# Retention plus Fourier mixing on one core: the order of seven products, and their sums and stores, in the last batch's second weight multiplication

## The chip, the core and the metric

The kernel runs on one core of a Trainium2 chip. A core has a matrix engine (TensorE, PE in the profile; its weight loads are PEld), three engines for element-wise work (VectorE is DVE, ScalarE is ACT, GpSimd is POOL), a fifth that mostly issues DMAs (SyncE, SP), a large on-chip memory (SBUF) and a small one into which TensorE accumulates (PSUM, in banks). Each engine works through its own queue in order and waits on semaphores for the others. POOL does not touch PSUM in this kernel. The metric is the time of one execution in microseconds (us); a kernel's time is the median of its runs.

## The reference

Two stages. The first is a linear attention with a decay per head, over 4 batches, 8 heads, 768 steps and head size 64; the second takes its output as 4 sequences of 768 rows of 512:

```python
for t in range(S):
    state = gamma * state + einsum('bhd,bhe->bhde', k[:, :, t], v[:, :, t])
    y[:, :, t] = scale * einsum('bhd,bhde->bhe', q[:, :, t], state)
...
X = np.fft.fft(np.fft.fft(x, axis=1), axis=2)
u = x + np.real(X)
un = (u - mean(u)) / sqrt(var(u) + 1e-06)
out = u + np.maximum(un @ w_ch1, 0.0) @ w_ch2
```

w_ch1 is 512 x 2048, w_ch2 is 2048 x 512. Only the last line, in the last of the four batches, is touched by the change: the multiplication of the hidden layer by w_ch2 and the adding of u.

## The kernel before

The batches go through a software pipeline: while one batch's feed-forward ("majors") runs on PE, the attention and the Fourier transforms of the next one are woven in between. `emit` (L1233) sorts the units of all streams by a due time between b and b+1 and traces them in that order; for each engine, the compiler keeps about that order and may take an instruction earlier when it reckons the one in front not to be ready.

In the last batch there is no next one. Its 768 rows are taken in three groups p = 0, 1, 2 of 256 rows, and each is 8 hidden units (`h3_unit`, L1032) and then 7 products (`p3_unit`, L1066): 45 majors, the n-th due at n/45 of the batch. Beside them run the last three row blocks (128 rows each) of the batch's own Fourier transform and norm, at the due times MIX3 (L40): `s2_unit` (matmuls L838, ACT copies L840 and L841, DVE L845 and L848, POOL L875 and L877), `norm_unit` (DVE bn_stats L895 and L896, a square root on ACT L898), `scaled_unit` (DVE L912 and L913, ACT L916) and `unT_unit` (a transposing DMA on SP, L938). Group 0 has the fifth row block's norm beside its products. The sixth block's `s2_unit` comes between group 0's last product and group 1's first hidden unit, its norm just ahead of group 1's third hidden unit.

A hidden unit n is 16 matmuls of 256 columns (L1039) into one of three PSUM banks (`ps_pm`) and a relu to f16 into `ht16`, rows n and n + 8: on ACT (L1044) for all n but 2, on DVE (L1046) for n = 2. After units 3 and 7 DVE makes four sums of hidden blocks each (L1063).

The multiplication by w_ch2 is done with seven products in place of eight quarter products. A group's hidden rows are A11, A12 (first 128 rows; first and second 1024 hidden columns) and A21, A22 (second 128 rows); w_ch2 is B11, B12, B21, B22 in the same way, each 1024 x 256. With

```
S1 = A21 + A22   S2 = S1 - A11   S3 = A11 - A21   S4 = A12 - S2
T1 = B12 - B11   T2 = B22 - T1   T3 = B22 - B12   T4 = B21 - T2
P1 = A11 B11   P2 = A12 B21   P3 = S4 B22   P4 = A22 T4   P5 = S1 T1   P6 = S2 T2   P7 = S3 T3
w = P1 + P6
o11 = u11 + P1 + P2            o12 = u12 + w + P5 + P3
o21 = u21 + w + P7 + P4        o22 = u22 + w + P7 + P5
```

S1 to S4 are the tiles `hsum` and T1 to T4 the tiles `wsum` (made once, ahead). Each product is 8 matmuls (L1096), weights from the hidden side. PSUM banks come from `ps_g` (5 banks): P1 and P2 accumulate in bank a, P5 and P3 in bank d; b, c and e are P6's, P7's and P4's.

The sums: w is copied from bank a by ACT (L1100) after P1; DVE adds P4 to u21 in place (L1115), P2 to u11 giving o11 (L1102), P6 to w (L1119); then POOL adds w to u22, u21 and u12 in place, in this order (L1121); DVE adds P5 to u22 in place (L1117), P7 to u22 and u21 giving o22 and o21 (L1123, L1124), and the content of d after P3 to u12 giving o12 (L1109). o11 and o12 are one tile of 512 columns, o21 and o22 another.

The order of the products is in `PROD` (L43): 1, 4, 2, 6, 5, 7, 3 in the first two groups, 1, 4, 6, 5, 7, 3, 2 in the last. In the last group bank a is two banks with 128 columns each: P1 and P2 are then 16 matmuls of 128 columns, with their ACT copy and DVE add in halves.

Stores: in the first two groups one of 512 columns for the first row block (L1113, after P3) and one for the second (L1125, after P7), on SP's queue. In the last group the second row block still goes in one piece (L1125), o12 on SP (L1111), and o11 in two halves, the first on ACT's queue and the second on SP's (L1105). L1331 holds the program's closing waits.

Of the kernel before, what the change touches and what calls it, by code (L numbers as in the profile page):

```python
# [12 lines left out]
ALU = mybir.AluOpType  # L13
# [5 lines left out]
P = 128  # L19
B, H, S, D = 4, 8, 768, 64  # L20
DM = 512
# [18 lines left out]
MIX3 = ((0.005, 0.035, 0.070, 0.105), (0.190, 0.310, 0.325, 0.350), (0.355, 0.395, 0.420, 0.470))  # L40
WS = (0.7, 1.05)
H3_ACT = (0, 1, 3, 4, 5, 6, 7)
PROD = ((1, 4, 2, 6, 5, 7, 3), (1, 4, 6, 5, 7, 3, 2))  # L43
HS_AT = {3: (0, 4), 7: (4, 8)}
ACT_ROWS = ((2, 5, 6, 7, 8, 9, 10, 14), (0, 3, 6, 7, 9, 10, 11, 12, 14, 15))

# [2 lines left out]
def kernel(  # L49
# [9 lines left out]
    nc = tc.nc  # L59
# [276 lines left out]
    for j in range(2):  # L336
        x = const.tile([P, NCH, 2, XW], f16, tag=f"x16_{j}", name=f"x16_{j}")
# [689 lines left out]
    def wsum(j, f):  # L1027
        return ws[j][:, f, :] if f < 6 else ws["hi", j // 2][:, 2 * (j % 2) + f - 6, :]
# [37 lines left out]
    def p3_unit(p, n):  # L1066
        def run():
            u = lb[B - 1]["u"]
            r0, r1 = 2 * p, 2 * p + 1
            u11, u12 = u[:, r0, 0:256], u[:, r0, 256:DM]  # L1070
            u21, u22 = u[:, r1, 0:256], u[:, r1, 256:DM]
            end = p == 2
            if n == 1:
                pr.clear()
                pr["o"] = [obp.tile([P, DM], f32, tag="ob", name="ob") for _ in range(2)]
                pr["w"] = inp.tile([P, 2, NCH, D], f32, tag="in32", name="ws32").rearrange(
                    "p a c d -> p (a c d)")[:, 0:256]
            o0, o1 = pr["o"]
            o11, o12, o21, o22 = o0[:, 0:256], o0[:, 256:DM], o1[:, 0:256], o1[:, 256:DM]
            w = pr["w"]  # L1080
            bank, first, last, lh, rh = {
                1: ("a", True, False, lambda f: ht16[:, f, 0:P], lambda f: w216[:, f, 0:256]),
                2: ("a", False, True, lambda f: ht16[:, 8 + f, 0:P],
                    lambda f: w216[:, 8 + f, 0:256]),
                3: ("d", False, True, lambda f: hs[3][:, f], lambda f: w216[:, 8 + f, 256:DM]),
                4: ("e", True, True, lambda f: ht16[:, 8 + f, P:256], lambda f: wsum(3, f)),
                5: ("d", True, False, lambda f: hs[0][:, f], lambda f: wsum(0, f)),
                6: ("b", True, True, lambda f: hs[1][:, f], lambda f: wsum(1, f)),
                7: ("c", True, True, lambda f: hs[2][:, f], lambda f: wsum(2, f))}[n]
            cols = ((0, 128), (128, 256)) if bank == "a" and end else ((0, 256),)  # L1090
            if first:
                pr[bank] = [ps_g.tile([P, 256], f32, tag="g", name="psc", padded_shape=[P, DM])
                            for _ in cols]
            for ps, (c0, c1) in zip(pr[bank], cols):
                for f in range(8):
                    nc.tensor.matmul(ps[:, c0:c1], lh(f), rh(f)[:, c0:c1],  # L1096
                                     start=first and f == 0, stop=last and f == 7,
                                     skip_group_check=True)
                if n == 1:
                    nc.scalar.copy(w[:, c0:c1], ps[:, c0:c1])  # L1100
                elif n == 2:
                    nc.vector.tensor_tensor(out=o11[:, c0:c1], in0=ps[:, c0:c1],  # L1102
                                            in1=u11[:, c0:c1], op=ALU.add)
                    if end:
                        (nc.sync if c0 else nc.scalar).dma_start(  # L1105
                            out[B - 1, r0 * P:r0 * P + P, c0:c1], o11[:, c0:c1])
            ps = pr[bank][0]
            if n == 3:
                nc.vector.tensor_tensor(out=o12, in0=ps, in1=u12, op=ALU.add)  # L1109
                if end:  # L1110
                    nc.sync.dma_start(out[B - 1, r0 * P:r0 * P + P, 256:DM], o12)  # L1111
                else:
                    nc.sync.dma_start(out[B - 1, r0 * P:r0 * P + P], o0)  # L1113
            elif n == 4:
                nc.vector.tensor_tensor(out=u21, in0=ps, in1=u21, op=ALU.add)  # L1115
            elif n == 5:
                nc.vector.tensor_tensor(out=u22, in0=ps, in1=u22, op=ALU.add)  # L1117
            elif n == 6:
                nc.vector.tensor_tensor(out=w, in0=ps, in1=w, op=ALU.add)  # L1119
                for x in (u22, u21, u12):  # L1120
                    nc.gpsimd.tensor_tensor(out=x, in0=x, in1=w, op=ALU.add)  # L1121
            elif n == 7:
                nc.vector.tensor_tensor(out=o22, in0=ps, in1=u22, op=ALU.add)  # L1123
                nc.vector.tensor_tensor(out=o21, in0=ps, in1=u21, op=ALU.add)  # L1124
                nc.sync.dma_start(out[B - 1, r1 * P:r1 * P + P], o1)  # L1125
        return run

    def w1_unit(g):
# [125 lines left out]
    for b in range(B):  # L1254
# [14 lines left out]
        else:  # L1269
            for p in range(3):  # L1270
                majors += [h3_unit(p, n) for n in range(8)]
                majors += [p3_unit(p, n) for n in PROD[p == 2]]
        streams.append((majors, b, b + 1.0))
# [8 lines left out]
        if b + 1 < B:  # L1282
# [7 lines left out]
            else:  # L1290
                streams.append(([load_unit(b + 1, i) for i in range(4)], b + LD1[0], b + LD1[1]))
                n = [len(u) for u in steps[1:]]
# [3 lines left out]
            end = b + ts[-1]  # L1296
# [39 lines left out]
```

## Time and profile before

| what | value |
|---|---|
| median of 3 runs | 247.41 us (246.95 to 247.58) |
| the profiled execution | 246.58 us |
| its span, first to last instruction | 244.8 us |
| granted TensorE clock | 1.000 over the span |
| the three runs of 8 hidden units (chain of waits) | 6.99, 6.99 and 7.00 us |
| group 0, 1, 2 of products, PE from P1's start to the last matmul's end | 206.56 to 213.48, 220.54 to 227.22, 234.04 to 240.99 us |
| last store: issue, landing | 241.34 us, 1.7 us later |

A timeline row gives the start, the length, the engine, the line, the operation, what it writes and reads, the shape and how many instructions were merged; in brackets is the time the engine stood idle before it, and what ended that. An engine name with a q is its queue issuing a DMA. PE's instructions overlap: a matmul lasts longer than the time after which the next may start. Times count from the span's start.

### The profile page before, as it was taken

Reading aid. Unit: us, or ns where it says so; the run is one execution under the profiler, and the core shown is the slowest. Engines: PE = TensorE matmul, PEld = TensorE weight load, DVE = VectorE, ACT = ScalarE, POOL = GpSimd, SP = SyncE. Lnnn points to the kernel's source line nnn. Section 1 sums busy time; section 2 is a strip of 40 time slices with the busy share of each in tenths; the row PEclk is TensorE's granted clock in tenths of the full one; section 3 lists DMA queues with packets and bytes.
Section 4 is the critical chain, followed back from the end, with each engine's and each line's share of the span. In section 5 each row is a group of like instructions: output and inputs, shape, how many; then the busy total and the mean of one; then the engine's idle time right before and its main releaser. Section 6 shows DMA issues by size and latency. Waiting matters only on the chain.

```text
span 244.8 us, 5672 instructions
## 1 busy us (share of the span) xinstructions
PE 232.4 (95%) x2160; PEld 156.2 (64%) x2160; DVE 190.7 (78%) x476; ACT 131.1 (54%) x287; POOL 87.8 (36%) x155
## 2 busy tenths in 40 slices
PE   6897899999999998999999999999999999999993
PEld 2454668956766645665567546665666469888882
DVE  8998958897797788996885778899896646865443
ACT  8798679587775444751247515732247527271330
POOL 7667601465600067690000646660003220522112
PEclk9999999999999999999999999999999999999999
DMA  8999999799999487999999467696200241031202
GB/s 176 258 259 144 200 200 203 176 250 266 251 215 225 72 171 176 191 177 149 253 277 215 93 151 201 122 121 139 88 0 1 62 134 21 3 112 21 86 3 87
DMA packets 99355, 36.41 MB, mean 149 GB/s; under 512 B 89856, under 2 KB 96384, under 8 KB 99328
## 3 DMA queue, kind: packets, MB, share of 16 engines
q1 hardware_dynamic: 94960, 31.79, 62.1%
q0 software_dynamic: 4224, 4.19, 10.7%
q8 instruction: 17, 0.28, 0.5%
q14 instruction: 10, 0.08, 0.1%
q10 hardware_dynamic: 144, 0.07, 0.1%
HBM read 27.26 MB, written 6.29 MB: 137 GB/s over the span
## 4 chain that ended last, share of the span: by engine, by line
PE 69%; DMA 8%; DVE 7%; ACT 6%; SPq 4%; POOL 3%; issue 2%; ACTq 0%; POOLq 0%; DVEq 0%
PE psc L997 21%; PE psh L958 18%; PE psh L1039 9%; PE psc L1096 6%; DMA q<-in_q_dram 5%; SPq L170 4%; PE ps L741 3%; PE wkA L605 3%; DMA k<-in_k_dram 3%; PE wkY L659 2%; PE pq L838 2%; PE wkY L655 1%; ACT un L891 1%; PE wkK L624 1%; ACT g L748 1%
## 5 line engine op out<-in xcount | busy, mean ns | idle before, releaser
L997 PE MATMUL psc<-w,ht 128*128 128x512 f16 x288 | 68.2, 379 | 0.0
L958 PE MATMUL psh<-unT,w 128*128 128x384 f16 x320 | 59.7, 326 | 0.0
L875 POOL TENSOR_TENSOR u<-u,x 128x256 f32<-128x256 f32 x21 | 13.4, 640 | 105.3 <-DVE u L845 97.1
L997 PEld LDWEIGHTS <-ht 128*128 128x128 f16 x288 | 27.2, 98 | 26.1 <-issue 0.2
L958 PEld LDWEIGHTS <-w 128*128 128x128 f16 x320 | 29.9, 98 | 15.8 <-issue 0.6
L962 ACT ACTIVATE ht<-psh 128x384 f16<-128x384 f32 x46 | 22.3, 490 | 23.6 <-PE psh L958 23.3
L608 DVE TENSOR_TENSOR atm<-wkA,maskp 128x512 f16<-128x512 f32 x36 | 23.7, 681 | 1.2 <-PE wkA L605 1.2
L1039 PE MATMUL psh<-unT,w 128*128 128x256 f16 x192 | 21.4, 273 | 0.0
L1039 PEld LDWEIGHTS <-w 128*128 128x128 f16 x192 | 18.7, 98 | 2.1
L964 DVE TENSOR_SCALAR ht<-psh 128x384 f16<-128x384 f32 x34 | 18.5, 547 | 1.8 <-PE psh L958 1.7
L895 DVE BATCH_NORM_STATS2 bst<-u 128x6 f32<-128x512 f32 x21 | 14.6, 695 | 6.6 <-POOL u L877 5.9
L1001 DVE SCALAR_TENSOR_TENSOR ob<-psc,stats,u 128x512 f32<-128x512 f32 x18 | 13.4, 744 | 6.5 <-PE psc L997 6.5
L634 DVE SCALAR_TENSOR_TENSOR s<-s,gk,wkK 128x128 f16<-128x128 f16 x48 | 16.3, 340 | 2.7 <-ACT s L630 1.9
L1044 ACT ACTIVATE ht<-psh 128x512 f16<-128x512 f32 x21 | 12.2, 593 | 10.5 <-PE psh L1039 10.4
L667 ACT ACTIVATE x<-wkY,gexp 128x384 f16<-128x384 f32 x24 | 12.8, 582 | 8.0 <-PE wkY L659 8.0
L902 ACT ACTIVATE un<-u,stats 128x512 f16<-128x512 f32 x15 | 10.8, 722 | 11.4 <-DVE stats L896 7.7
L388 POOL TENSOR_SCALAR kd<-k,gexp 128x384 f16<-128x384 f32 x24 | 13.9, 590 | 4.0 <-DMA k<-in_k_dram 4.0
L156 PE MATMUL wps<-ht 128*128 128x512 f16 x40 | 13.1, 433 | 2.2 <-POOL ht L207 2.2
L877 POOL TENSOR_TENSOR u<-u,x 128x256 f32<-128x256 f32 x21 | 13.3, 635 | 3.0 <-DVE stats L896 3.0
L1121 POOL TENSOR_TENSOR u<-u,ws 128x256 f32<-128x256 f32 x9 | 6.3, 728 | 20.6 <-DVE ws L1119 20.6
L605 PE MATMUL wkA<-qTz,kT 128*128 128x256 f16 x72 | 13.4, 273 | 0.1
L840 ACT COPY qn<-pq 128x128 f32<-128x128 f32 x18 | 4.9, 273 | 12.6 <-PE pq L838 12.6
(192 smaller groups left out, 430.3 us busy)
## 6 DMA issues: line engine op xcount, KB each, us to landing
q<-in_q_dram SPq DMA_DIRECT2D x16, 384.0 KB, 6.0
k<-in_k_dram SPq DMA_DIRECT2D x16, 384.0 KB, 5.6
v<-in_v_dram SPq DMA_DIRECT2D x16, 384.0 KB, 6.4
out_dram<-ob SPq DMA_DIRECT2D x23, 256.0 KB, 2.4
w<-in_moe_w_ch_dram POOLq DMA_DIRECT2D x8, 512.0 KB, 11.0
unT<-un SPq DMA_TRANSPOSE x15, 2.4
qTz<-q16z SPq DMA_TRANSPOSE x8, 3.9
kT<-kd SPq DMA_TRANSPOSE x8, 3.1
```

The lines of the kernel that those rows point to most:

```text
L388: kc = nc.gpsimd.tensor_scalar(out=kd[:, :, h2, :], in0=k32[:, h2], scalar1=gkd[:, h0 + h2:h0 + h2 + 1], scalar2=1.0, op0=ALU.mult, op1=AL ...
L605: mm = nc.tensor.matmul(wk[:, c2], st["kT"][:, c, :], st["qT"][:, :, c, :], start=True, stop=True)
L608: nc.vector.tensor_tensor(out=st["atm"][:, 2 * part:2 * part + 2], in0=wk, in1=maskp[:, PAIR_ORDER[i]].unsqueeze(1).to_broadcast([P, 2, 2, ...
L634: nc.vector.scalar_tensor_tensor(out=s16[:, c], in0=s16[:, c - 1], scalar=gk2[:, hp:hp + 1], in1=wk[:, c - c0], op0=ALU.mult, op1=ALU.add)
L875: nc.gpsimd.tensor_tensor(out=u[:, kb, 0:256], in0=u[:, kb, 0:256], in1=x[:, kb, 0, 1:257], op=ALU.add)
L895: nc.vector.bn_stats(bst, u[:, kb, :])
L958: nc.tensor.matmul(psh, w116[:, cb, fb * P:(fb + 1) * P], unT[:, cb, rt * 384:(rt + 1) * 384], start=(cb == 0), stop=(cb == 3))
L962: nc.scalar.activation(ht16[:, fb, :], psh, AF.Relu, bias=0.0, scale=-1.0)
L964: nc.vector.tensor_scalar(out=ht16[:, fb, :], in0=psh, scalar1=-1.0, scalar2=0.0, op0=ALU.mult, op1=ALU.max)
L997: nc.tensor.matmul(psc, ht16[:, fb, rb3 * P:(rb3 + 1) * P], w216[:, fb, :], start=(fb == 0), stop=(fb == NFB - 1))
L1039: nc.tensor.matmul(psh[:, t], w116[:, cb, fb * P:(fb + 1) * P], unT[:, cb, p * 256:(p + 1) * 256], start=(cb == 0), stop=(cb == 3))
L1096: nc.tensor.matmul(ps[:, c0:c1], lh(f), rh(f)[:, c0:c1], start=first and f == 0, stop=last and f == 7, skip_group_check=True)
```

## The change

The orders become 1, 4, 2, 5, 6, 7, 3 in the first two groups (P5 ahead of P6) and 1, 4, 6, 7, 5, 2, 3 in the last (P7 ahead of P5, P2 ahead of P3). In the last group it is now bank d that is in two halves, so P5 and P3 go in 16 matmuls of 128 columns with their DVE adds in halves, and P1 and P2 in 8 of 256. There DVE adds w to u22, where POOL did (POOL keeps u21 and u12), P7 is added to u22 in place, and o22 comes from P5. The last group's quarters are stored one by one: o21 after P7, o22 after P5, o11 after P2 on SP's queue, o12 after P3 in two halves, the first on ACT's queue and the second on SP's. `add` and `store` are new helpers for the same DVE add and DMA as before.

```diff
-PROD = ((1, 4, 2, 6, 5, 7, 3), (1, 4, 6, 5, 7, 3, 2))
+PROD = ((1, 4, 2, 5, 6, 7, 3), (1, 4, 6, 7, 5, 2, 3))
...
-            cols = ((0, 128), (128, 256)) if bank == "a" and end else ((0, 256),)
+            cols = ((0, 128), (128, 256)) if bank == "d" and end else ((0, 256),)
...
+            def add(o, x, y):
+                nc.vector.tensor_tensor(out=o, in0=x, in1=y, op=ALU.add)
+
+            def store(r, c0, c1, src, queue=nc.sync):
+                queue.dma_start(out[B - 1, r * P:r * P + P, c0:c1], src)
+
             for ps, (c0, c1) in zip(pr[bank], cols):
                 for f in range(8):
                     nc.tensor.matmul(ps[:, c0:c1], lh(f), rh(f)[:, c0:c1],
                                      start=first and f == 0, stop=last and f == 7,
                                      skip_group_check=True)
-                if n == 1:
-                    nc.scalar.copy(w[:, c0:c1], ps[:, c0:c1])
-                elif n == 2:
-                    nc.vector.tensor_tensor(out=o11[:, c0:c1], in0=ps[:, c0:c1],
-                                            in1=u11[:, c0:c1], op=ALU.add)
+                if n == 3:
+                    add(o12[:, c0:c1], ps[:, c0:c1], u12[:, c0:c1])
                     if end:
-                        (nc.sync if c0 else nc.scalar).dma_start(
-                            out[B - 1, r0 * P:r0 * P + P, c0:c1], o11[:, c0:c1])
+                        store(r0, 256 + c0, 256 + c1, o12[:, c0:c1], nc.sync if c0 else nc.scalar)
+                elif n == 5:
+                    add((o22 if end else u22)[:, c0:c1], ps[:, c0:c1], u22[:, c0:c1])
             ps = pr[bank][0]
-            if n == 3:
-                nc.vector.tensor_tensor(out=o12, in0=ps, in1=u12, op=ALU.add)
+            if n == 1:
+                nc.scalar.copy(w, ps)
+            elif n == 2:
+                add(o11, ps, u11)
                 if end:
-                    nc.sync.dma_start(out[B - 1, r0 * P:r0 * P + P, 256:DM], o12)
-                else:
-                    nc.sync.dma_start(out[B - 1, r0 * P:r0 * P + P], o0)
+                    store(r0, 0, 256, o11)
             elif n == 4:
-                nc.vector.tensor_tensor(out=u21, in0=ps, in1=u21, op=ALU.add)
-            elif n == 5:
-                nc.vector.tensor_tensor(out=u22, in0=ps, in1=u22, op=ALU.add)
+                add(u21, ps, u21)
             elif n == 6:
-                nc.vector.tensor_tensor(out=w, in0=ps, in1=w, op=ALU.add)
-                for x in (u22, u21, u12):
+                add(w, ps, w)
+                if end:
+                    add(u22, u22, w)
+                for x in (u21, u12) if end else (u22, u21, u12):
                     nc.gpsimd.tensor_tensor(out=x, in0=x, in1=w, op=ALU.add)
             elif n == 7:
-                nc.vector.tensor_tensor(out=o22, in0=ps, in1=u22, op=ALU.add)
-                nc.vector.tensor_tensor(out=o21, in0=ps, in1=u21, op=ALU.add)
-                nc.sync.dma_start(out[B - 1, r1 * P:r1 * P + P], o1)
+                add(u22 if end else o22, ps, u22)
+                add(o21, ps, u21)
+                if end:
+                    store(r1, 0, 256, o21)
+                else:
+                    store(r1, 0, DM, o1)
+            if n == 3 and not end:
+                store(r0, 0, DM, o0)
+            elif n == 5 and end:
+                store(r1, 256, DM, o22)
```

## The prediction

> **What bounds the kernel now.** First the page, to see which engine sets the time.
>
> ```profile
> span 244.8 us, 5672 instructions
> PE 232.4 (95%) x2160; PEld 156.2 (64%) x2160; DVE 190.7 (78%) x476; ACT 131.1 (54%) x287; POOL 87.8 (36%) x155
> PE 69%; DMA 8%; DVE 7%; ACT 6%; SPq 4%; POOL 3%; issue 2%; ACTq 0%; POOLq 0%; DVEq 0%
> ```
>
> TensorE (PE) is busy for 95% of the span and most of the chain that ended last. So I looked for where that chain leaves PE inside the three groups of products. Second view: the chain in order of time (start, length, what), L1096 being the products.
>
> ```profile
> 211.97 0.44 DVE u L1117
> 212.45 1.03 PE psc L1096 x8
> ...
> 225.71 0.44 DVE u L1117
> 226.19 1.03 PE psc L1096 x8
> ...
> 234.30 0.61 ACT ht L1044
> 234.96 1.87 PE psc L1096 x18
> ...
> 237.25 0.44 DVE ws L1119
> 237.82 0.74 POOL u L1121
> 238.58 0.44 DVE u L1117
> 239.06 1.94 PE psc L1096 x24
> 241.02 0.29 DVE ob L1102
> ```
>
> The same place stands in all three groups: L1117, VectorE's (DVE's) u22 += P5, just ahead of P3. P3 accumulates into the bank that L1117 reads, and L1117 works in place on u22, to which GpSimd (POOL) must first have added w (L1121). So PE waits for P6, the sum w, a POOL add and a DVE add. The last group has a second exit: ACT's relu (L1044) in front of P1.
>
> How long PE stands is read from the timeline. First group, with the DVE work around it:
>
> ```profile
> 209.17 2.78 PE L1096 MATMUL psc<-wsum,hsum 128*128 128x256 f16 x24
> 210.12 0.69 DVE L895 BATCH_NORM_STATS2 bst<-u 128x6 f32<-128x512 f32 x1
> 210.72 0.41 DVE L1119 TENSOR_TENSOR ws<-psc,ws 128x256 f32<-128x256 f32 x1
> 211.21 2.10 POOL L1121 TENSOR_TENSOR u<-u,ws 128x256 f32<-128x256 f32 x3 [1.13 <-DVE ws L1119]
> 212.31 0.33 DVE L913 SCALAR_TENSOR_TENSOR stats<-stats 128x1 f32<-128x1 f32 x1
> 213.55 7.15 PE L1039 MATMUL psh<-unT,w 128*128 128x256 f16 x64
> 213.59 0.42 DVE L1109 TENSOR_TENSOR ob<-psc,u 128x256 f32<-128x256 f32 x1 [0.29 <-PE psc L1096]
> 214.42 0.48 DVE L845 SCALAR_TENSOR_TENSOR u<-pq,g,qn 128x256 f32<-128x256 f32 x1 [0.40 <-ACT qn L841]
> 217.07 0.66 DVE L1046 TENSOR_SCALAR ht<-psh 128x512 f16<-128x512 f32 x1
> ```
>
> The first row is P6, P5 and P7 in one run of 24 matmuls. A matmul of 256 columns lasts 0.27 but the next starts before it ends: (2.78 - 0.27)/23 = 0.109 from start to start, so 0.87 per product, its result 0.16 after its slot. P3 was due at 209.17 + 2.62 = 211.79 and began at 212.45: **0.66 lost**.
>
> **The change, part by part.**
>
> *P5 ahead of P6 (first and second group).* The number of matmuls stays. L1117 moves ahead of the three POOL adds in u22's order, so it no longer waits for POOL; it runs when P5 ends, a product and more before P3 is due. The stall of P3 goes whole: 0.66 in the first group. In the second:
>
> ```profile
> 220.54 1.20 PE L1096 MATMUL psc<-w,ht 128*128 128x256 f16 x8
> 221.57 1.04 PE L1096 MATMUL psc<-wsum,ht 128*128 128x256 f16 x8
> 223.32 2.78 PE L1096 MATMUL psc<-wsum,hsum 128*128 128x256 f16 x24
> ```
>
> P3 was due at 223.32 + 2.62 = 225.94 and began at 226.19: 0.25.
>
> What is late next is the rest of P6's work, since P6 is now a product later while P3 is not. In the first group P6 ends at 210.92 + 0.16 = 211.08; DVE has bn_stats (210.12 to 210.81), then L1117 and then w, which ends at about 211.55 where L1119 ended at 211.13. POOL's three adds follow 0.08 behind, 211.63 to 213.73. o12 (L1109) needs the third of them and so runs from 213.77 to 214.19, while P3 ends about 212.8. Behind o12 on DVE stand L845, L848, then bn_stats of the row block in work (through POOL's L875 and L877), then the relu L1046 of the next hidden units. L845 could start at 214.42 - 0.66 = 213.76, but DVE takes it at 214.11 (one add starts about 0.34 behind another, as 239.09 and 239.44 in the rows of the last group below): this chain moves up 0.31, PE moves up 0.66. Hidden unit 2 is the relu's, and its bank (3 of them) is needed by unit 5. Before: relu ended 217.73, unit 5 was due at 213.55 + 40 x 0.109 = 217.92. After: relu ends 217.42, unit 5 is due at 217.26 and gets the bank at about 217.45. So 0.19 of the 0.66 is given back: **first group -0.47**.
>
> In the second group no row block is in work beside it. w ends about 225.75, POOL's adds 227.93, o12 228.37; the next DVE relu is not ready before 226.81 + 2.62 + 0.16 = 229.6. Nothing is given back: **-0.25**.
>
> *Last group.* Rows:
>
> ```profile
> 235.25 1.04 PE L1096 MATMUL psc<-wsum,ht 128*128 128x256 f16 x8
> 236.12 2.78 PE L1096 MATMUL psc<-wsum,hsum 128*128 128x256 f16 x24
> 239.09 0.42 DVE L1123 TENSOR_TENSOR ob<-psc,u 128x256 f32<-128x256 f32 x1
> 239.44 0.41 DVE L1124 TENSOR_TENSOR ob<-psc,u 128x256 f32<-128x256 f32 x1
> 239.93 1.06 PE L1096 MATMUL psc<-w,ht 128*128 128x128 f16 x16
> 241.34 0.33 SPq L1105 DMA_DIRECT2D out_dram<-ob  x1
> ```
>
> P1 loses its halves. The matmul of its last hidden block waits for the relu of 234.30 to 234.90, and in halves several matmuls still stand behind that wait: P4 began at 235.25. Whole, as in the second group, P1's last matmul starts at the release (there 220.54 + 1.20 - 0.28 = 221.46) and P4 0.11 behind (221.57). Here that is 234.96 + 0.11 = 235.07: **-0.18**.
>
> P5 and P3 get the halves. Sixteen of 128 columns take 1.06 - 0.22 = 0.84 for fifteen steps, 0.056 each, 0.90 a product against 0.87; two products gain halves and two lose them: **0**.
>
> P3 was due at 236.12 + 2.62 = 238.74 and began at 239.06: 0.32. With the new order P6 runs 235.94 to 236.81, P7 to 237.68, P5 to 238.58, P2 to 239.45, and P3 is due then. DVE: w 237.07 to 237.49; u22 += w, new on DVE, 237.58 to 238.01; u22 += P7 238.10 to 238.52 (a DVE add that uses the one before starts 0.09 after its end: L1117, 0.42 from 238.58, and the add of 239.09); o21, which waits for POOL's u21 (237.64 to 238.36), 238.44 to 238.86; the two adds of P5, 238.78 to 239.29. P3's first half needs the first of these, done 239.07, and is due 239.45: the stall goes, **-0.32**, with 0.38 to spare. The added wait is o21's for POOL; queued behind it on DVE are P5's adds, and P3 waits for these, so that 0.38 is its cover.
>
> The price of u22 += w (two f32 operands in SBUF, 128x256) has no row: 0.29 at least (the 128-column add L1102), 0.69 at most (bn_stats over 512 f32), 0.42 taken, as all 256-column adds here. At 0.69 the slack is 0.11, at 0.29 it is 0.51. Neither enters the sum.
>
> The end keeps its form: a last half of 128 columns, its DVE add, a store on SP. Four stores become five, o21 and o22 go out at about 238.9 and 239.3, o11 at 240.2, P3's first half on ACT's queue. SP issues take 0.33 each, so SP is free before the last one, at about 240.87.
>
> ```profile
> out_dram<-ob SPq DMA_DIRECT2D x1, 64.0 KB, 1.7
> out_dram<-ob SPq DMA_DIRECT2D x23, 256.0 KB, 2.4
> ```
>
> The last store is again 64 KB: 1.7 from issue to landing, taken as unchanged. If the fifth store ahead of it cost it something, the bound is the 2.4 of the whole-row stores, +0.7; nothing speaks for a gain there.
>
> *One rule that speaks against the change.* What this trace has of DVE and POOL adding at once:
>
> ```profile
> 208.56 0.41 DVE L1063 TENSOR_TENSOR hsum<-ht,hsum 128x512 f16<-128x512 f16 x1
> 208.72 0.74 POOL L875 TENSOR_TENSOR u<-u,x 128x256 f32<-128x256 f32 x1 [6.92 <-DVE u L845]
> L875 POOL TENSOR_TENSOR u<-u,x 128x256 f32<-128x256 f32 x21 | 13.4, 640 | 105.3 <-DVE u L845 97.1
> ```
>
> A POOL add that began inside a DVE add of two SBUF operands took 0.74 where the 21 average 0.64. The Trainium skill ("SBUF — State Buffer", section "SBUF: two separate sides") says that a DVE instruction with two SBUF inputs and a GpSimd one that reads SBUF exclude each other for their whole length. By that the new DVE add (start 237.58) holds back POOL's u21 (start 237.64) by up to 0.42; the row agrees in sign, and shows 0.10.
>
> In numbers of the rows alone: with u21 0.42 later, o21 starts about 238.83, P5's first add ends 239.46, and P3 would start 0.05 behind at 239.5, a stall of 0.05. With 0.10 there is none. I take none.
>
> **The sum.** -0.47 - 0.25 - 0.18 - 0.32 = -1.22 against the profiled execution, 246.58 (span 244.8 and 1.8 around it): span 243.6, execution 245.4. That execution is 0.83 below the median of the three runs and below their lowest (246.95), so I apply the difference to the median: 247.41 - 1.2 = **246.2**.
>
> **Rivals.**
>
> *Nothing given back.* DVE's order is not the program's: in the first group bn_stats ran ahead of w though it stands behind it in the program. If L845 or the relu comes ahead of o12, the 0.19 stays: -1.41, 246.0.
>
> *The first group's gain is hidden anyway.* If the chain behind o12 ends where it did (217.73 for the relu), unit 5 waits for it 0.50 and, as ACT's relus are queued behind its square root of the same chain, the rest may go too: -0.75, 246.7. For it: unit 5 had its bank only 0.19 early. Against it: L845 can move up by 0.31.
>
> *POOL gets there first in the last group.* If POOL's u21 starts before u22 += w and shuts it out until 238.36, that add ends 238.82, u22 += P7 239.33, o21 239.67, P5's first add 239.88, and P3 starts 239.93, a stall of 0.48: the last group gives 0.02, the total is -0.74, 246.7. Against it: DVE follows its own result by 0.09, POOL that of DVE by 0.15 (237.82 behind 237.25 + 0.42). The skill's rule named above is what would make the later of the two wait whole.
>
> *It does not do what it says.* The compiled order puts P3 or its add where they still wait, and only P1's part is left: -0.2, 247.2.
>
> *Slower.* Place: the bank of hidden unit 5 in the second group. DVE is in order, and w may come behind the norm of the row block in work, whose last small operation (L913) ran at 212.31. Then w ends at 212.7 (1.6 later than before), POOL's adds 214.9, o12 215.35, L845 starts 215.27 (0.85 later), the relu ends 218.58, and unit 5, due 217.26, waits 1.35: -0.66 + 1.35 - 0.75 = -0.06. It decides from there: each 0.1 more is 0.1 slower. With o12 one add later still it is +0.35, 247.8. Against it: w ran ahead of that operation before.
>
> **Chances.** Forecast 0.40; nothing given back 0.19; first group hidden 0.17; POOL first 0.06; not as it says 0.08; slower 0.10. 0.3% is 0.74, about what a measurement of this kernel can tell from no change. Faster by more: the first two and something under half of the two at -0.75, 0.67. Within: 0.23. Slower: 0.10. Range: from 246.0 less half the spread of the three runs (0.3), 245.6, up to the case where only P1's part is left, 247.2; the unknown prices (0.05 for the shut-out; 0.7 for the last landing, which still gives 246.9) lie inside.
>
> **What would show it.** Right: in the timeline in the first two groups P3's row starts 2.62 behind the row of three products, with no wait in brackets; L1117's counterpart waits for PE alone; POOL's three adds begin 0.4 later in the first group, and o12 waits for POOL; P4 of the last group begins 0.11 after P1's release; the last DVE add ends about 0.47 nearer to that release's relu than now (241.31 - 234.90 = 6.41, to about 5.9). Wrong: PE waits for a relu in the second group's hidden units by more than 0.3; P3 of the last group waits for a DVE add; the last store lands later than 1.7 from issue; or PE's time before 206 differs, which no step here touches.

## The result, and the profile after

| | before | after |
|---|---|---|
| median of 12 runs, same chip | 246.94 us | 245.85 us |
| ratio to before, 95% interval | | 0.9956 (0.994 to 0.9973) |
| profiled execution, its span | 246.58, 244.8 us | 245.54, 243.8 us |

1.09 us faster, 0.44%, with a 95% interval of 0.67 to 1.48; 1.2 was forecast. The two profiled executions differ by 1.04 and their spans by 0.97, so the stages below add up to 0.97 and not to 1.09. The rows of the page after that answer the ones shown before:

```profile
span 243.8 us, 5673 instructions
PE 77%; DVE 6%; ACT 5%; SPq 4%; DMA 3%; issue 2%; POOL 1%; ACTq 0%; POOLq 0%
L1039 PE MATMUL psh<-unT,w 128*128 128x256 f16 x192 | 21.6, 272 | 0.6 <-DVE ht L1046 0.6
```

PE's share of the chain went up from 69% to 77%. But PE now stands idle for 0.6 in front of one of the hidden units (L1039), until DVE's relu (L1046) ends. The chain of waits in order of time shows where (start, length, what; the products are L1103 now):

```profile
206.66 6.11 PE psc L1103 x56
...
213.97 0.61 ACT ht L1044
214.63 0.49 DVE u L845
215.19 0.64 POOL u L875
215.82 0.60 POOL u L877
216.45 0.70 DVE bst L895
217.36 0.58 DVE ht L1046
217.99 2.78 PE psh L1039 x24
220.77 6.27 PE psc L1103 x56
227.04 6.99 PE psh L1039 x64
234.03 6.33 PE psc L1103 x72
240.38 0.29 DVE ob L1096
```

Each group of products is now one unbroken run on PE: the exits over L1117, L1119 and L1121 are gone. In their place the chain leaves PE once, in the second group's hidden units, through the sixth row block (L845, L875, L877, bn_stats) and the relu behind it. A hidden unit is 8 matmuls of 256 columns (two halves of four, 64 in a run of eight units; the 16 given with the kernel before is wrong, and the forecast's 40 matmuls ahead of unit 5 count 8 each). PE gets back with three units left (x24), so it is unit 5 that waited. The timeline around it:

```profile
210.06 0.69 DVE L895 BATCH_NORM_STATS2 bst<-u 128x6 f32<-128x512 f32 x1
211.53 0.17 DVE L912 RECIPROCAL stats<-stats 128x1 f32<-128x1 f32 x1 [0.36 <-ACT stats L898]
211.61 0.41 DVE L1096 TENSOR_TENSOR ws<-psc,ws 128x256 f32<-128x256 f32 x1
211.74 1.04 PE L1103 MATMUL psc<-w,hsum 128*128 128x256 f16 x8
212.16 2.10 POOL L1126 TENSOR_TENSOR u<-u,ws 128x256 f32<-128x256 f32 x3 [2.13 <-DVE stats L913]
214.29 0.42 DVE L1096 TENSOR_TENSOR ob<-psc,u 128x256 f32<-128x256 f32 x1 [0.26 <-POOL u L1126]
214.63 0.47 DVE L845 SCALAR_TENSOR_TENSOR u<-pq,g,qn 128x256 f32<-128x256 f32 x1
217.28 0.66 DVE L1046 TENSOR_SCALAR ht<-psh 128x512 f16<-128x512 f32 x1
217.99 0.71 PE L1039 MATMUL psh<-unT,w 128*128 128x256 f16 x5 [0.62 <-DVE ht L1046]
```

P3 (211.74) starts on time. Unit 5 was due at 217.21 (one unit of 0.87 behind 216.33, the start of unit 4) and started at 217.99, 0.78 late, when the relu had ended at 217.94. (The 0.62 in the brackets is less because it counts from the end of the matmul in front, and matmuls overlap.) The last group:

```profile
233.86 1.20 PE L1103 MATMUL psc<-w,ht 128*128 128x256 f16 x8
234.12 0.60 ACT L1044 ACTIVATE ht<-psh 128x512 f16<-128x512 f32 x1 [0.28 <-PE psh L1039]
234.90 1.04 PE L1103 MATMUL psc<-wsum,ht 128*128 128x256 f16 x8
237.36 0.43 DVE L1096 TENSOR_TENSOR u<-u,ws 128x256 f32<-128x256 f32 x1
237.40 1.65 POOL L1126 TENSOR_TENSOR u<-u,ws 128x256 f32<-128x256 f32 x2 [9.42 <-DVE ws L1096]
238.41 0.82 DVE L1096 TENSOR_TENSOR ob<-psc,u 128x256 f32<-128x256 f32 x3
239.28 1.06 PE L1103 MATMUL psc<-w,hsum 128*128 128x128 f16 x16
```

P3 (239.28) follows P2 with no wait; the row of 238.41 is o21 and the two halves of P5's add. From the end of the last relu to the end of the last DVE add it is 5.95 (234.72 to 240.67), where it was 6.41.

Stage by stage (first P1 at 206.56 before, 206.50 after):

| stretch | before | after | difference |
|---|---|---|---|
| span's start to the first P1 | 206.56 | 206.50 | -0.06 |
| first P1 to second group's P1 (first group and the hidden units behind it) | 13.98 | 14.11 | +0.12 |
| to the last group's P1 | 13.51 | 13.26 | -0.25 |
| to the end of the last add | 7.27 | 6.80 | -0.47 |
| to the span's end | 3.48 | 3.15 | -0.33 |

(Differences from unrounded times.) The two first groups together gained only 0.12 of the 0.72 forecast; the end behind the last add gave 0.33 that was not forecast.

### The profile page after: what moved, and what is told of

It reads as the page before. It is cut to its first block, busy times and chain, and to the rows that moved or that the text cites. A ratio compares the mean times of both kernels' runs of the same rounds, so it can differ in the third digit from the quotient of the medians.

```text
span 243.8 us, 5673 instructions
## 1 busy us (share of the span) xinstructions
PE 232.4 (95%) x2160; PEld 156.3 (64%) x2160; DVE 191.1 (78%) x478; ACT 130.9 (54%) x286; POOL 87.2 (36%) x154
## 4 chain that ended last, share of the span: by engine, by line
PE 77%; DVE 6%; ACT 5%; SPq 4%; DMA 3%; issue 2%; POOL 1%; ACTq 0%; POOLq 0%
PE psc L997 25%; PE psh L958 19%; PE psc L1103 8%; PE psh L1039 7%; SPq L170 4%; PE wkA L605 3%; DMA q<-in_q_dram 3%; PE psh L975 3%; PE ps L741 3%; PE wkY L659 2%; PE pq L838 2%; PE wkY L655 1%; PE tq L561 1%; PE wkK L624 1%; ACT g L748 1%
## 5 line engine op out<-in xcount | busy, mean ns | idle before, releaser
L875 POOL TENSOR_TENSOR u<-u,x 128x256 f32<-128x256 f32 x21 | 13.4, 640 | 104.6 <-DVE u L845 95.2
L1039 PE MATMUL psh<-unT,w 128*128 128x256 f16 x192 | 21.6, 272 | 0.6 <-DVE ht L1046 0.6
L1039 PEld LDWEIGHTS <-w 128*128 128x128 f16 x192 | 18.7, 98 | 2.9 <-issue 0.8
L877 POOL TENSOR_TENSOR u<-u,x 128x256 f32<-128x256 f32 x21 | 13.3, 635 | 3.0 <-DVE stats L896 1.2
L1126 POOL TENSOR_TENSOR u<-u,ws 128x256 f32<-128x256 f32 x8 | 5.8, 756 | 21.0 <-DVE ws L1096 18.9
L975 PE MATMUL psh<-unT,w 128*128 128x128 f16 x192 | 11.5, 219 | 0.1
```

What stands on the lines that cost most here:

```text
L975: mm = nc.tensor.matmul(psh[:, f], w116[:, cb, fb * P:(fb + 1) * P], unT[:, cb, kb * P:(kb + 1) * P], start=(cb == 0), stop=(cb == 3))
L1039: nc.tensor.matmul(psh[:, t], w116[:, cb, fb * P:(fb + 1) * P], unT[:, cb, p * 256:(p + 1) * 256], start=(cb == 0), stop=(cb == 3))
```

## The experiments

The time ahead of the first P1, which no kernel here touches, lies between 206.4 and 207.3 over the profiles. So beside each ratio to the kernel before stands the stretch from the first P1's start to the last DVE add's end, from each profile. Kernels whose stretch is the same, 34.17 to 34.18, have ratios from 0.995 to 0.9972: the ratio alone does not tell such small differences apart, and the argument goes by the stretch.

| kernel | ratio to before (95%) | stretch, us |
|---|---|---|
| before | | 34.76 |
| changed | 0.9956 (0.994 to 0.9973) | 34.17 |
| new order in the first two groups only | 0.9995 (0.9983 to 1.0006) | 34.64 |
| last group only | 0.9972 (0.996 to 0.9984) | 34.30 |
| norm due behind unit 2 | 0.9956 (0.994 to 0.9973) | 34.18 |
| norm due behind all hidden units | 0.995 (0.9936 to 0.9965) | 34.17 |
| norm held behind unit 2's relu | 0.9934 (0.9921 to 0.9946) | 33.39 |
| norm held behind unit 7's relu | 0.9942 (0.9928 to 0.9957) | 33.39 |
| u22 on GpSimd | 0.9986 (0.9977 to 0.9995) | 34.41 |
| four stores | 0.9972 (0.9963 to 0.9982) | 34.18 |
| P5 and P3 whole | 0.9975 (0.9966 to 0.9984) | 34.33 |
| w ahead of the reciprocal | 0.9947 (0.9933 to 0.9961) | 33.64 |
| P1's eighth matmul late, all groups | 0.9938 (0.9925 to 0.9952) | 33.44 |
| the same, last group only | 0.9932 (0.9918 to 0.9945) | 33.23 |

**The two halves of the change by themselves.** On the kernel before:

```diff
-PROD = ((1, 4, 2, 6, 5, 7, 3), (1, 4, 6, 5, 7, 3, 2))
+PROD = ((1, 4, 2, 5, 6, 7, 3), (1, 4, 6, 5, 7, 3, 2))
```

> The kernel before with the new order in the first two groups alone; the last group, its sums and its stores as before. Theory A (the first group's gain is given back, because VectorE's relu of hidden unit 2 in the second group comes too late): P3 starts without a wait in both groups (0.66 and 0.25 gained), and unit 5 of the second group waits about 0.78 for that relu, so 0.25 - 0.12 = 0.13 us faster than before, span 244.7. The prediction's sum (0.19 given back): 0.72 faster, span 244.1.

And on the changed kernel, the old order in the first two groups:

```diff
-PROD = ((1, 4, 2, 5, 6, 7, 3), (1, 4, 6, 7, 5, 2, 3))
+PROD = ((1, 4, 2, 6, 5, 7, 3), (1, 4, 6, 7, 5, 2, 3))
```

> The changed kernel with the old order in the first two groups; only the last group is new. Theory A: P3 waits 0.66 and 0.25 again and no hidden unit waits; the last group gives 0.46 from its relu to its last add, and the end behind it about 0.3 (a shorter landing and closing), so about 0.8 faster than before, span 244.0, and 0.1 to 0.2 slower than the changed kernel. If the end behind the last add is chance: 0.5 faster, span 244.3.

Timeline of the first kernel, P3 and then the hidden units:

```profile
212.00 1.04 PE L1096 MATMUL psc<-w,hsum 128*128 128x256 f16 x8
218.25 2.78 PE L1039 MATMUL psh<-unT,w 128*128 128x256 f16 x24 [0.62 <-DVE ht L1046]
```

and of the second:

```profile
212.32 1.03 PE L1103 MATMUL psc<-w,hsum 128*128 128x256 f16 x8 [0.50 <-DVE u L1096]
213.42 7.15 PE L1039 MATMUL psh<-unT,w 128*128 128x256 f16 x64
```

With the new order P3 is on time and unit 5 waits; with the old one P3 waits and all 64 matmuls of the hidden units are one run. So the gain of the first group and its loss belong to the same edit: the first two groups' new order moves the stretch by 0.11 and the ratio by nothing that can be told from 1. Most of the gain is the last group's: 0.46 of the 0.59 by which the changed kernel's stretch is shorter. Its ratio, 0.9972, shows a gain by itself; that it is less than the changed kernel's 0.9956 is not shown by the ratios, whose intervals overlap.

**Does a later due time move the wait?** In the changed kernel the sixth row block's norm was made due later.

```diff
-MIX3 = (..., (0.355, 0.395, 0.420, 0.470))
+MIX3 = (..., (0.355, 0.405, 0.420, 0.470))
```

> The changed kernel with the sixth row block's norm due 0.405 in place of 0.395, so that it is traced behind hidden unit 2 and its relu, not ahead of it. Theory A (VectorE's order alone): the relu of unit 2 starts at about 215.7, unit 5 does not wait, and all of 0.78 is gained: span about 243.0. Theory B (ScalarE's queue is as late: its relu of unit 3 is behind the square root, that of unit 4 behind the normalised row block): the wait moves from unit 5 to unit 6 or 7 and is 0.6 to 0.75 there, so at most 0.15 is gained: span 243.7.

```diff
+MIX3 = (..., (0.355, 0.515, 0.540, 0.560))
```

> The changed kernel with the sixth row block's norm, scaling and transpose due 0.515, 0.540 and 0.560, behind all hidden units of the second group. Theories A and B both: no hidden unit of the second group waits, 0.75 gained over the changed kernel, span about 243.0, about 1.8 faster than before. If the norm, late, holds VectorE's or ScalarE's work of the second group's products, or its transposed rows come too late for the third group's hidden units (needed at about 226.1), part of it is lost there.

Neither told the theories apart, since the order on VectorE and ScalarE stayed what it was: the compiler took the norm forward again, and unit 5 waited 0.79 and 0.78. They serve as two repeats of the changed kernel (stretch 34.18 and 34.17).

**The norm held by an order dependency.** The same due times, 0.405 for the first and 0.515, 0.540 and 0.560 for the second, with bn_stats and the rest of `norm_unit` for that block tied behind the relu of unit 2 (`relu[p, n]` is the instruction that `h3_unit` makes):

```diff
+    def behind_relu(unit, *which):
+        def run():
+            with ExitStack() as held_back:
+                for x in which:
+                    held_back.enter_context(tc.issue_after(relu[x]))
+                unit()
+        return run
...
+                if kb == 5:
+                    fs[1] = behind_relu(fs[1], (1, 2))
```

> The changed kernel with the norm of the sixth row block held behind VectorE's relu of hidden unit 2 of the second group by an order dependency (a later due time alone left the compiled order as it was). Theory A (the lost 0.78 is this place in VectorE's order): the relu starts at about 215.7 in place of 217.28, unit 5 does not wait, and 0.6 to 0.78 is gained over the changed kernel: span 243.0 to 243.2. Theory B (ScalarE's queue, with the square root and the normalised row block in it, is as late): the wait moves to unit 6 or 7 and at most 0.15 is gained: span 243.7.

and with norm and scaling behind the relu of unit 7 too:

```diff
+                if kb == 5:
+                    fs[1:3] = [behind_relu(f, (1, 2), (1, 7)) for f in fs[1:3]]
```

> The same with the norm and scaling of the sixth row block on ScalarE held behind the relu of hidden unit 7 as well, so that ScalarE does nothing but relus in the second group. Theories A and B both: no hidden unit of the second group waits, 0.78 gained over the changed kernel, span 243.0. If the late row block costs something in its turn (ScalarE's copy of P1 behind the square root, VectorE's small operations among the sums, the transposed rows later than about 226 where the third group's hidden units start), that much less.

The first one's timeline, and its chain from the first group's end:

```profile
215.61 0.69 DVE L1046 TENSOR_SCALAR ht<-psh 128x512 f16<-128x512 f32 x1 [0.16 <-PE psh L1039]
216.40 0.69 DVE L895 BATCH_NORM_STATS2 bst<-u 128x6 f32<-128x512 f32 x1
217.35 0.29 ACT L898 ACTIVATE stats<-stats,epsT 128x1 f32<-128x1 f32 x1 [0.20 <-DVE stats L896]
```

```profile
212.96 6.99 PE psh L1039 x64
219.94 6.27 PE psc L1104 x56
226.21 6.99 PE psh L1039 x64
233.20 6.33 PE psc L1104 x72
```

The relu starts at 215.61, as soon as unit 2 is there, the eight units are one run of 6.99, and 0.78 is gained. bn_stats started no later for it (216.40, against 216.45): it had waited for GpSimd all along, and kept the ready relu behind it. Theory B falls: ScalarE's square root and scaling still stand among its relus, and no hidden unit waits. Taking them out as well gives the same stretch, 33.39.

**The pair that made w late.** In the changed kernel, one exchange on VectorE: `scaled_unit` of the fifth block, that is L912 and L913 on VectorE and L916 on ScalarE behind them, is tied behind the first group's add of w (`pr["w of", 0]` is that add).

```diff
+    def behind_w(unit):
+        def run():
+            with tc.issue_after(pr["w of", 0]):
+                unit()
+        return run
...
+                if kb == 4:
+                    fs[2] = behind_w(fs[2])
```

> The changed kernel with one pair of VectorE instructions exchanged by an order dependency: in the first group the sum w stands ahead of the reciprocal (L912) that waits for ScalarE's square root, where the compiler had put it behind. Theory (the prediction's working was right but for this pair, which made w 0.5 late): w ends at about 211.5, GpSimd's adds at 213.7, o12 at 214.2, and the relu of unit 2 at 217.4; unit 5 waits 0.2 in place of 0.78, the 0.19 that the prediction gave: span 243.2 to 243.3. Rival (something else holds o12 or the relu): the wait stays above 0.5, span 243.6 or more.

```profile
211.39 0.42 DVE L1096 TENSOR_TENSOR ws<-psc,ws 128x256 f32<-128x256 f32 x1
211.77 0.16 DVE L912 RECIPROCAL stats<-stats 128x1 f32<-128x1 f32 x1
211.89 2.09 POOL L1126 TENSOR_TENSOR u<-u,ws 128x256 f32<-128x256 f32 x3 [1.61 <-DVE ws L1096]
211.97 0.66 DVE L913 SCALAR_TENSOR_TENSOR stats<-stats 128x1 f32<-128x1 f32 x1
217.00 0.66 DVE L1046 TENSOR_SCALAR ht<-psh 128x512 f16<-128x512 f32 x1
```

This execution runs 0.25 later than the changed kernel's in front of the groups. Taking that off, w ends 0.46 earlier, the relu 0.53 earlier, and unit 5 waits 0.25 in place of 0.78; the stretch is 0.53 shorter. Expected was a wait of 0.2. The span, 243.7, missed the expected 243.2 to 243.3: 0.25 of that is the later start, and 0.18 a longer closing behind the last store.

**The last group's parts.** w added to u22 on GpSimd again:

```diff
                 add(w, ps, w)
-                if end:
-                    add(u22, u22, w)
-                for x in (u21, u12) if end else (u22, u21, u12):
+                for x in (u22, u21, u12):
```

> The changed kernel with the last group's addition of w to u22 back on GpSimd, ahead of u21 and u12. Theory (the add on VectorE is what lets P3 start on time): o21 then waits for GpSimd's second add, at 238.85 in place of 238.37; the adds of P5 behind it on VectorE end at about 239.5, and P3 of the last group starts at about 239.57 in place of 239.28: 0.28 slower than the changed kernel, span 244.1. Rival (VectorE's add shuts GpSimd out, so nothing was won): no difference, span 243.8.

```profile
237.45 2.10 POOL L1124 TENSOR_TENSOR u<-u,ws 128x256 f32<-128x256 f32 x3 [9.42 <-DVE ws L1096]
238.90 1.15 DVE L1096 TENSOR_TENSOR ob<-psc,u 128x256 f32<-128x256 f32 x4 [0.26 <-POOL u L1124]
239.57 1.05 PE L1103 MATMUL psc<-w,hsum 128*128 128x128 f16 x16
```

o21 (238.90) waits for GpSimd's second add, P5's adds stand behind it, and P3 starts at 239.57, 0.24 after it was due. So the DVE add is part of the gain: without it 0.24 of the 0.32 that P3 gained would be lost again, and 0.08 left.

One store fewer, and P5 and P3 whole:

```diff
                 add(o21, ps, u21)
-                if end:
-                    store(r1, 0, 256, o21)
-                else:
+                if not end:
                     store(r1, 0, DM, o1)
...
-                store(r1, 256, DM, o22)
+                store(r1, 0, DM, o1)
```

> The changed kernel with the last row block stored in one piece after P5, so four stores in the last group as before the change. Theory (the end behind the last store is shorter because the fifth store moves the last one a place on in the closing waits, 0.06 each): the last add and its store stay, the closing is 0.06 longer, span 243.9. Rival (the smaller stores land sooner and so give the 0.10 shorter landing): the last store's landing is 1.67 again, span 244.0.

```diff
-            cols = ((0, 128), (128, 256)) if bank == "d" and end else ((0, 256),)
+            cols = ((0, 128), (128, 256)) if bank == "z" and end else ((0, 256),)
...
-                        store(r0, 256 + c0, 256 + c1, o12[:, c0:c1], nc.sync if c0 else nc.scalar)
+                        store(r0, 256 + c0, 256 + c1, o12[:, c0:c1], nc.sync)
```

No bank is called "z", so nothing is in halves.

> The changed kernel without halves in the last group: P5 and P3 are 8 matmuls of 256 columns each, with one DVE add, and o12 is one store of 128 KB on SP. Theory (the halves are worth their overlap at the very end, since P3 comes last): the products end 0.05 earlier, but the last add is 0.42 long in place of 0.29 and begins only at P3's end, and the store is twice as large: the last add ends 0.1 later, and its store lands in about 1.7 in place of 1.57, so 0.2 slower than the changed kernel, span 244.0. Rival (halves cost as much in matmuls and issues as they hide): no difference, span 243.8.

With four stores the stretch is the same, the last store lands 1.57 after its issue as with five (1.67 before the change), and the closing behind it (from that landing to the end of the span) is 1.62 in place of 1.56. That difference alone would not do, since the closing of kernels with five stores goes from 1.56 to 1.74. But SyncE's closing waits are about 0.06 apart, and behind the last landing eight of them stand with four stores (here and in the kernel before) and seven with five, one having passed 0.30 ahead of it: that is the 0.06 expected. The rival, that smaller stores land sooner, falls. The span of 244.4 against 243.9 expected is a first P1 that is 0.48 later. With P5 and P3 whole the last add ends 0.16 later, counted from the first P1, and its store of 128 KB lands in 1.69, 0.12 later: 0.28, where 0.2 was expected.

**A little more.** In the kernel with the norm behind unit 2's relu, P1's matmul that waits for unit 7 was put behind seven of P4, first in all groups, then in the last alone (there with the condition `end`, as shown):

```diff
-                for f in range(8):
+                def mm(f):
...
+                for f in range(8):
+                    if end and n == 1 and f == 7:
+                        pr["late"] = mm
+                        continue
+                    if end and n == 4 and f == 7:
+                        pr["late"](7)
+                        nc.scalar.copy(w, pr["a"][0])
+                    mm(f)
...
-            if n == 1:
+            if n == 1 and not end:
                 nc.scalar.copy(w, ps)
```

> The kernel of the run before with the norm held behind the relu of unit 2, and in each group P1's eighth matmul (the one that waits for the relu of hidden unit 7) put behind seven matmuls of P4. Theory (that wait, 0.15 a group, is all that TensorE still loses between hidden units and products): groups 1 and 2 each gain about 0.15 and group 0, which has other matmuls there, up to 0.04; span 242.7 against 243.0. Rival (the ACT copy of P1, 0.9 later, or the sums S2 and S3 then hold P6 or P7): the wait comes back there, span 243.0.

> The kernel with the norm held behind the relu of unit 2, and P1's eighth matmul behind seven of P4 in the last group alone, where P6 and P7 stand between P4 and P2 and so the copy of P1 is not waited for. Theory: 0.16 from the last relu to the last add, as in the run with all groups, and nothing lost in groups 0 and 1: span 242.85 against 243.0. Rival: the sums or the copy hold P6: span 243.0.

The first one's timeline in the first group:

```profile
208.94 0.49 PE L1104 MATMUL psc<-wsum,hsum 128*128 128x256 f16 x3
209.03 0.37 ACT L1114 COPY ws<-psc 128x256 f32<-128x256 f32 x1 [0.93 <-PE psc L1104]
209.46 1.03 PE L1104 MATMUL psc<-w,ht 128*128 128x256 f16 x8
```

P2 accumulates on P1, so it waits for ScalarE's copy of P1, which is now late; the compiler has pulled three matmuls of P5 ahead of it, and still 0.19 is lost. In the second group the expected 0.15 did not come either (0.02 was lost). In the last group P6 and P7 stand between, nothing waits, and 0.16 is gained. So the rival held in the first group and the theory in the last, and in the last group alone the stretch is 33.23, the shortest. The ratios 0.9934 and 0.9932 of the two best kernels can't be told apart. By the stretch both are faster than the changed kernel, by 0.78 and 0.94, and the tie of bn_stats behind one relu brings 0.78 of it; by the ratios, the first one's interval overlaps the changed kernel's (0.994 to 0.9973) a little and the second one's reaches 0.9945.

## Why the prediction was right, and where it was not

- **P3's stalls in the first two groups go**: right, both. The second group, -0.25 forecast, gave -0.25.
- **0.19 of the first group's 0.66 is given back**: wrong, 0.78 was; a wait for that relu of more than 0.3 was one of the prediction's own signs of being wrong. The place was right (the bank of unit 5, held by unit 2's relu, behind bn_stats, GpSimd's adds, L845 and o12). The step that failed is "DVE has bn_stats (210.12 to 210.81), then L1117 and then w, which ends at about 211.55". Between them the compiled order put the reciprocal L912, and that waits for ScalarE's square root: w ended at 212.02. Every later time is then the forecast one plus about 0.5: o12 214.72 for 214.19, L845 214.63 for 214.11, the relu's end 217.94 for 217.42. Exchanging that one pair brought the wait to 0.25, near the 0.19, so that is shown. So in the first two groups the rival "the first group's gain is hidden anyway" came true and not the forecast. It did so by the lateness of w that the slower rival had named: w came 0.9 later than before, where the forecast had 0.4 and the slower rival 1.6.
- **P1 whole, -0.18**: P4 began 0.18 behind the last relu where it had been 0.35: -0.17.
- **P3 of the last group, -0.32**: it starts as due. Its cover was 0.38 by forecast and 0.26 in the trace (P5's first add ended at 239.03).
- **u22 += w on VectorE**: 0.43 for the 0.42 taken. GpSimd's add beside it took 0.97 (the two are 1.65 together, the second 0.72), and o21 began 3.69 behind the last relu (238.41), 0.15 later than forecast, which is about what the cover lost. By the rule of the Trainium skill that was weighed ("SBUF — State Buffer", section "SBUF: two separate sides"), GpSimd would have been held for the whole 0.38 left of the DVE add; it took 0.24 longer, between the row's 0.10 and that, and P3 did not wait.
- **The end keeps its form**: wrong by 0.33. Landing 0.10 and closing 0.23 shorter. Of the closing, 0.06 is the fifth store (shown by the four-store kernel); the rest varies from profile to profile (1.56 to 1.74 with the new last group, 1.69 and 1.78 with the old one). So 0.16 of the 0.33 comes with the new last group, and the other 0.17 is no more than this variation. Why the last 64 KB land in 1.57 with the new last group and in 1.66 and 1.67 with the old one stays open; the number of stores is not it.

So it is in part luck that the forecast of -1.2 came near the measured -1.09. In the two profiled spans (-0.97) the 0.59 too much in the first group and 0.04 in the last stand against 0.33 at the end and 0.06 ahead of the groups that were not forecast. The stretch, which the forecast was about, became 0.59 shorter and not 1.22: that is nearer the rival's -0.75 than the forecast. The measured interval, 0.67 to 1.48, has room for both.

## What to carry to other kernels

When a stall on the matrix engine is removed, look up the margin of the next shared buffer (here a bank with 0.19 to spare) and the whole in-order queue that frees it: what did not move with the matrix engine can now be late there. An instruction that is ready, but stands behind one that waits for a third engine, was cheap to fix here: the norm's statistics lost nothing behind the relu, and 0.78 came back. A due time is only a wish if the compiler may look ahead: check the compiled order of each queue, and tie the pair that matters.

## What the runs showed of the hardware

VectorE's L913, an operation on one element per partition that reads two operands from SBUF, takes 0.15 to 0.16 with GpSimd idle. In four kernels it began inside one of GpSimd's adds, and each time it ended about 0.015 behind that add: in the kernel with w ahead of the reciprocal it began at 211.97, inside the first add (211.89 to 212.61), and took 0.66; with P1's eighth matmul late in all groups it took 0.57, in the kernel before 0.33, and with the last group alone new 0.32. The reciprocal L912, which reads one operand, took 0.16 inside such an add as without one. The other way round, GpSimd's add that began 0.04 behind VectorE's u22 += w took 0.97, where the next one took 0.72.
